# A layer-norm, attention and mixer kernel on one core: the first layer norms staggered by half tiles, segment sums moved from TensorE to VectorE, fewer columns in a product, another last store

## The chip, the cores and the metric

The kernel runs on one core of a Trainium2 chip. The metric is the device time of one execution in microseconds (us). Executions of one kernel spread by a few us (1528.29 to 1531.67 for the kernel before); medians of several are quoted, with the smallest and largest. A profiled execution has a "span", which is about 2 us shorter than the time that the same execution reports (1527.2 against 1529.11 us in the profile before). Runs that lie over 1.5% above the fastest of their kernel would be classed as slow and kept apart.

Engines are named as the profile names them: PE is TensorE (matrix products), PEld its weight loads, DVE is VectorE, ACT is ScalarE, POOL is GpSimd, SP is SyncE, which here only issues DMAs. A "q" after an engine ("SPq", "ACTq") is its queue of DMA issues.

## The reference, cut to what matters

```python
xn = layernorm(x)                                  # x: 2048 x 1024, bf16
out = x + A(xn, mem0, Wq, Wk, Wv, Wo) + B(xn, w1, w2, w3, w4)

def A(x, mem, ...):                                # 64 segments of 32 tokens, 32 heads of 128
    for s in range(64):
        h = concat([mem, x[32*s : 32*s+32]])       # 8 memory rows ahead of 32 tokens
        o = attention(h) @ Wo                      # causal for tokens; memory rows see all 40 rows
        mem = o[:8]                                # the next segment's memory
        outs.append(o[8:])

def B(x, w1, w2, w3, w4):
    h  = gelu(layernorm(x) @ w1)
    hs = shift_four_groups(h) @ w2                 # quarters of h shifted by -1, +1, -2, +2 tokens
    x1 = x + hs
    return x1 + gelu(layernorm(x1) @ w3) @ w4      # 3584 hidden columns
```

The loop over segments is serial. The kernel speculates: attention weights of memory rows are nearly uniform for such data, so the next memory is approximated by the mean of the values of a segment. That mean needs the *sum of the normalised rows of each segment* ("segment sums"), times Wv ("mean-value product"), times Wo ("G product"). All segments then run in parallel, and a test at the end (with a serial loop behind it, which does not run here) guards the guess.

## The kernel before

TensorE runs through these stages (starts on the PE timeline, us): first product with w1 from 9.5; shift product with w2 from 75.1; w3 product from 130.1 and w4 product from 178.9, which alternate in four blocks of 512 tokens; between their groups the mean-value and G products from 203.0; the V product from 542.6; attention from 763.6, that is Q and K projections with small score and output products between; output products to 1521.7.

The loads at the front, and the statistics of a tile (128 rows) for the layer norm of a layer norm:

```python
load_x(0); load_x(1)                       # 256 KB each, SyncE's queue
for c in range(2):                         # w1 in halves
    nc.sync.dma_start(w1_sb[:, :, c * 512:(c + 1) * 512], w1_v[:, :, c * 512:(c + 1) * 512])
    load_x(c + 2)
...
nc.vector.bn_stats(st[:, 0, :], xt[:, 0:512])         # part 0
nc.vector.bn_stats(st[:, 1, :], xt[:, 512:1024])
nc.vector.bn_aggr(mv[:], st[:])
nc.vector.tensor_scalar(ab[:, 0:1], mv[:, 1:2], EPS, None, op0=ALU.add)
nc.vector.tensor_scalar(ab[:, 1:2], ab[:, 0:1], EPS, mv[:, 1:2], op0=ALU.mult, op1=ALU.add)
nc.gpsimd.tensor_tensor(rr[:], ab[:], neghalf[:], op=ALU.pow)
```

The first eight tiles are transposed on TensorE, the others by transposing DMAs. The segment sums are TensorE products too, eight of four columns for each of the 16 tiles:

```python
def seg_sums(n, xn):
    ps = psum0.tile([P, KT, 4], F32, tag="xs")
    for k in range(KT):
        nc.tensor.matmul(ps[:, k, :], xn[:, k * P:(k + 1) * P], segsum[:], start=True, stop=True)
    nc.scalar.copy(xsum[:, :, 4 * n:4 * n + 4], ps[:])
```

The mean-value product works on 71 columns, for the first segment has eight memory rows that all get one value (NQ = 7 + 64):

```python
for hh in range(4):
    for k in range(KT):
        nc.tensor.matmul(ps[:, hh, :], wv[:, k, hh * P:(hh + 1) * P], xb[:, k, :NQ], start=(k == 0), stop=(k == KT - 1))
```

In the w4 stage each tile needs its residual R1 (loaded from memory, x added by POOL, then added to the product by VectorE):

```python
for j in range(4):
    R1, xt = r1s.pop(n); load_r1(n + 1)                        # SyncE's queue
    nc.gpsimd.tensor_tensor(R1[:], R1[:], xt[:], op=ALU.add)
    for ch in range(2):
        ...28 matmuls of 512 columns...
        nc.vector.tensor_tensor(R1[:, half], ps[:], R1[:, half], op=ALU.add)
    # [after tile 0: mean-value products begin]
```

The attention weights Pn of each tile are transposed by a DMA of SyncE's queue into PT. That queue also brings the weights Wq and Wk and the values V, issued in the order of the program. The output product of a tile is scheduled 10 units of the schedule's own clock (roughly us) after its scores:

```python
nc.sync.dma_start_transpose(PTr, Pn[:rows].rearrange("p h k -> p (h k)"))   # 176 of them
...
LAT = 10.0
smalls.append((clock[0] + LAT, ("O", gi_), o_item))
```

The last output is 512 columns wide: an addition by VectorE and a store of 128 KB by SyncE's queue.

Of the kernel before, what the change touches and what calls it, by code (L numbers as in the profile page):

```python
# [77 lines left out]
def kernel(  # L78
# [39 lines left out]

    def const_tile(name, arr):
        d = nc.inline_tensor(_bf(arr), name=name)  # L120
        t = cpool.tile(list(arr.shape), BF16, name=name + "_sb")
        nc.gpsimd.dma_start(t[:], d.ap())
        return t

    ident = const_tile("c_ident", np.eye(P, dtype=np.float32))
    segsum_np = np.zeros((P, 4), np.float32)
    for t in range(P):
        segsum_np[t, t // SEG] = 1.0
    segsum = const_tile("c_segsum", segsum_np)
# [11 lines left out]
    nc.vector.memset(neghalf[:], -0.5)  # L141
    sums = cpool.tile([P, NTILE * 8, 4], F32)
# [41 lines left out]
    with tc.manual_schedule(engines={mybir.EngineType.PE, mybir.EngineType.SP, mybir.EngineType.Pool}), ExitStack() as actx:  # L184
# [6 lines left out]
        with ExitStack() as bctx:  # L191
            w3ctx = bctx.enter_context(ExitStack())
            xctx = bctx.enter_context(ExitStack())
            xsum = xctx.enter_context(tc.tile_pool(name="xs", bufs=1)).tile([P, KT, NSEG], BF16)
# [12 lines left out]
            with ExitStack() as hctx:  # L207
# [7 lines left out]
                with ExitStack() as p0:  # L215
# [13 lines left out]
                    load_x(1)  # L229
                    for c in range(2):  # L230
                        nc.sync.dma_start(w1_sb[:, :, c * 512:(c + 1) * 512], w1_v[:, :, c * 512:(c + 1) * 512])
                        load_x(c + 2)
                    for n in range(4, 7):
                        load_x(n)
# [5 lines left out]
                    def norm_stats(n, part=None):  # L240
# [13 lines left out]
                        nc.vector.tensor_scalar(ab[:, 0:1], mv[:, 1:2], EPS, None, op0=ALU.add)  # L254
                        nc.vector.tensor_scalar(ab[:, 1:2], ab[:, 0:1], EPS, mv[:, 1:2], op0=ALU.mult, op1=ALU.add)
# [4 lines left out]
                    def norm2(n, xn2T, jj):  # L260
                        st, mv, ab, rr, nm2 = stats[n]
                        xn2 = ring.tile([P, D], BF16, tag="xn2")
                        if n < NPE:
                            nc.vector.tensor_scalar(xn2[:], xts[n][:], mv[:, 0:1], rr[:, 1:2], op0=ALU.subtract, op1=ALU.mult)
                        else:
                            nc.scalar.activation(xn2[:], xts[n][:], ACTF.Identity, bias=nm2[:], scale=rr[:, 1:2])
                            nc.sync.dma_start_transpose(xn2T[:, jj], xn2[:])
# [21 lines left out]
                    def seg_sums(n, xn):  # L289
                        ps = psum0.tile([P, KT, 4], F32, tag="xs")  # L290
                        for k in range(KT):
                            nc.tensor.matmul(ps[:, k, :], xn[:, k * P:(k + 1) * P], segsum[:], start=True, stop=True)  # L292
                        nc.scalar.copy(xsum[:, :, 4 * n:4 * n + 4], ps[:])

                    def stage1(n0, nt, xn2T, between):
                        w = nt * P
                        for co in range(KT):
                            ps = psum.tile([P, 512], F32, tag="mm", bufs=4)
                            for k in range(KT):
                                nc.tensor.matmul(ps[:, :w].rearrange("p (n t) -> p n t", t=P), w1_sb[:, k, co * P:(co + 1) * P],  # L300
                                                 xn2T[:, :nt, k, :], start=(k == 0), stop=(k == KT - 1))
# [14 lines left out]
                    for i in range(13):  # L316
                        nc.tensor.matmul(ps[:], wz[:, :P], wz[:], start=(i == 0), stop=(i == 12))
                    norm_stats(0)
                    norm_stats(1, 0)
                    t0 = xn2T_tile()  # L320
                    xn2 = norm2(0, t0, 0)
                    transposes(xn2, t0, 0, 0)
                    transposes(xn2, t0, 0, 1, on_dve=True)
# [3 lines left out]
                    t1 = xn2T_tile()  # L327
                    xn2 = norm2(1, t1, 0)
                    norm_stats(2)

                    def first(xn2=xn2, t1=t1):
                        transposes(xn2, t1, 0, 0)
                        transposes(xn2, t1, 0, 1)
                    xns = {}

                    def sums_of(n):
                        if n in xns:
                            seg_sums(n, xns.pop(n))

                    stage1(0, 1, t0, {3: [first], 4: [lambda: norm_stats(3)]})  # L340
                    groups = [(1, 1)] + [(n, 2) for n in range(2, NT, 2)]
                    tiles2 = {1: t1}
                    xn2s = {}

                    def prep(n):
                        xn2s[n] = norm2(n, tiles2[n - n % 2], n % 2)
                        norm_stats(n + 2)
                        done = range(n - 2, n - 1) if n < NPE else range(NPE - 2, n + 1) if n == NPE else range(n, n + 1)
                        for m in done:
                            xns[m] = norm1(m)  # L350

                    def tr(n, half):
                        transposes(xn2s[n], tiles2[n - n % 2], n % 2, half)


                    for gi, (n0, nt) in enumerate(groups):
                        between = {c: [] for c in range(KT)}
                        if gi + 1 < len(groups) and groups[gi + 1][0] < NPE:
                            m0 = groups[gi + 1][0]
                            tiles2[m0] = xn2T_tile()  # L360
                            prep(m0)
                            between[1] += [lambda m0=m0: tr(m0, 0), lambda m0=m0: prep(m0 + 1)]
                            between[2] += [lambda m0=m0: tr(m0, 1)]
                            between[5] += [lambda m0=m0: tr(m0 + 1, 0)]
                            between[6] += [lambda m0=m0: tr(m0 + 1, 1)]
                        if gi + 2 < len(groups) and groups[gi + 2][0] >= NPE:
                            m0 = groups[gi + 2][0]
                            tiles2[m0] = xn2T_tile()
                            between[2] += [lambda m0=m0: prep(m0)]
                            between[5] += [lambda m0=m0: prep(m0 + 1)]  # L370
                        between[3] += [lambda n0=n0: sums_of(n0 - 1)]
                        between[4] += [lambda n0=n0: sums_of(n0 - 2)]
                        stage1(n0, nt, tiles2[n0], between)
                    for n in range(NT):
                        sums_of(n)
# [29 lines left out]
            with ExitStack() as p3:  # L405
# [5 lines left out]
                m0 = ring.tile([M, D], BF16, tag="m0", bufs=1)  # L411
                nc.sync.dma_start(m0[:], A_mem0[0])
                for _ in range(4):
                    load_w3()
                for c in range(7):
                    nc.sync.dma_start(w4_sb[:, 4 * c:4 * (c + 1), :], w4_v[:, 4 * c:4 * (c + 1), :])

                vbT = big.tile([P, H, NQ + 1], BF16)
                xb = big.tile([P, KT, NQ + 1], BF16)
                gps = []  # L420

                def mem_start():
# [4 lines left out]
                    t0 = ring.tile([P, KT, 1], F32, tag="t0", bufs=1)  # L427
                    nc.vector.tensor_tensor(t0[:], ps9[:, :, M:M + 1], xsum[:, :, 0:1], op=ALU.add)
                    nc.vector.tensor_copy(xb[:, :, 8:NQ], xsum[:, :, 1:NSEG])
# [88 lines left out]
                for tb in range(4):  # L518
# [18 lines left out]
                    for j in range(4):  # L537
# [17 lines left out]
                        if n == NT - 2:  # L555
                            load_wv()
# [440 lines left out]
```

## Time and profile before

| | before |
|---|---|
| time, median of 3 runs | 1529.53 us (1528.29 to 1531.67) |
| span of the profiled run | 1527.2 us |
| PE busy | 1512.6 us, 99% |
| waits of PE in all | about 6 us, nearly all before 20 us |

The engines' busy times on the page of the kernel before (busy us, share of the span, number of instructions):

```profile
PE 1512.6 (99%) x9810; PEld 810.3 (53%) x9883; DVE 530.1 (35%) x1131; ACT 506.8 (33%) x1155; POOL 178.8 (12%) x248
```

TensorE is nearly always busy, so only what shortens its own stream or its waits can show. The waits of PE before (what waited <- engine and tile that ended the wait: us in total, times, longest):

```profile
PE ps L300 <- DMA w_sb<-in_B_w_dram: 2.0, 1, 2.0
PE ps L283 <- DVE xn L264: 1.3, 1, 1.3
...
PE ps L292 <- DVE xnk L273: 0.7, 1, 0.7
```

They are the first half of w1, the first normalised tile, and a segment sum that waits for its input (the line left out is a wait of the warm-up matmuls at the start, of 1.3 us). There is no wait at all for w4. The third cost of the front is the clock. The windows of the kernel before (stretch, length, busy us of each engine, granted TensorE clock, DMA share, GB/s):

```profile
core 0: us, PE busy (x) PEld busy (x) DVE busy (x) ACT busy (x) POOL busy (x), PEclk, DMA share, GB/s
8.00:10.00 2.00, 0.45 (x8) 0.46 (x9) 1.42 (x5) 0.00 (x0) 0.40 (x1) 1.00 1.08 378
10.00:12.00 2.00, 2.00 (x30) 2.00 (x27) 1.66 (x3) 0.83 (x3) 0.40 (x3) 0.69 1.09 394
12.00:14.00 2.00, 1.99 (x20) 1.72 (x19) 1.10 (x5) 1.35 (x3) 0.69 (x1) 0.50 1.06 408
```

PE idled for 2 us until 9.55, and from about 10.8 to 14.2 it ran at half clock (the granted clock was 0.77 from 10.5 to 11.0, 0.50 from 11.0 to 14.0 and 0.82 from 14.0 to 14.5). Before that PE had waited 1.35 us for the first normalised tile and 2.04 us for w1, with eight transposes (0.62 us) between.

Lines of the timeline before (start, us, engine, line, operation): a group of segment sums and what follows it, a group of mean-value products and what follows it, and the tail.

```profile
48.42 0.34 PE L292 MATMUL ps<-c_segsum_sb,xnk 128*128 128x4 bf16 x8
48.62 1.03 PE L300 MATMUL ps<-xn2T,w_sb 128*128 128x256 bf16 x8
...
203.04 1.20 PE L440 MATMUL ps<-xb,wt 128*128 128x71 bf16 x32
204.07 2.11 PE L548 MATMUL ps<-w_sb,h3T 128*128 128x512 bf16 x8
...
1522.16 0.69 DVE L716 TENSOR_TENSOR ot<-pso,Rt 128x512 bf16<-128x512 f32 x1 [6.21 <-PE pso L710]
1522.88 0.36 SPq L717 DMA_DIRECT2D out_dram<-ot  x1
```

Matmuls overlap (the group of segment sums at 48.42 us lasts 0.34 us, and the next work starts 0.20 us after it began), so what a group costs is read from its start to the next start, not from its duration: 0.20 us for a group of segment sums (26 ns for each four-column matmul), 1.03 us for 32 matmuls of 71 columns. From the start of the last addition to the end of the span (1527.2) there are 5.04 us.

### The profile page before, as it was taken

To read this page: it belongs to the slowest core of one execution; us is meant where nothing else is said; L and a number is where in the kernel's file an instruction comes from. 1 tells how busy PE (TensorE), PEld (TensorE's weight loads), DVE (VectorE), ACT (ScalarE), POOL (GpSimd) and SP (SyncE) were. 2 spreads that over 40 slices of the span, in tenths; PEclk is the share of its full clock that TensorE was granted. 3 is DMA by queue.
4 is the path that set the end of the run, shared out by engine and by line. 5 is a ranking of instruction groups with operands and counts; after the bars stand their busy time and mean duration, and the time that the engine had idled before them with its cause. 6 is when DMAs were issued, how large, how long until landed. Compare 5 with 4: busy or idle time off the path is not lost.

```text
span 1527.2 us, 24314 instructions
## 1 busy us (share of the span) xinstructions
PE 1512.6 (99%) x9810; PEld 810.3 (53%) x9883; DVE 530.1 (35%) x1131; ACT 506.8 (33%) x1155; POOL 178.8 (12%) x248
## 2 busy tenths in 40 slices
PE   8999999999999999999999999999999999999998
PEld 7844444444444444444466645654665555445554
DVE  8284010000210122211146624650664266426641
ACT  5533202103012011111156614650663266326620
POOL 5232020221211222100000010001000100010001
PEclk9999999999999999999999999999999999999999
DMA  8679543452352877632399947992997389728611
GB/s 252 186 221 308 208 158 118 142 183 90 115 176 80 213 259 255 223 123 82 125 242 247 235 133 183 234 244 74 229 251 187 106 222 227 183 80 203 177 46 51
DMA packets 287373, 270.03 MB, mean 177 GB/s; under 512 B 136875, under 2 KB 255040, under 8 KB 287000
## 3 DMA queue, kind: packets, MB, share of 16 engines
q1 hardware_dynamic: 265208, 185.79, 47.5%
q0 software_dynamic: 22048, 82.63, 15.5%
q8 instruction: 80, 1.31, 0.4%
q14 instruction: 37, 0.30, 0.1%
HBM read 190.98 MB, written 46.19 MB: 155 GB/s over the span
## 4 chain that ended last, share of the span: by engine, by line
PE 98%; DMA 1%; DVE 0%; issue 0%; ACT 0%; SPq 0%
PE ps L652 30%; PE ps L579 14%; PE pso L710 14%; PE ps L523 13%; PE ps L548 13%; PE ps L387 4%; PE ps L300 3%; PE psS L667 2%; PE psO L691 2%; DMA xt<-in_A_x_dram 1%; PE ps L474 1%; PE ps L837 1%; PE ps L440 1%; PE gps L454 1%; PE ps L292 0%
## 5 line engine op out<-in xcount | busy, mean ns | idle before, releaser
L652 PE MATMUL ps<-hTb,wt 128*128 128x396 bf16 (+3 forms) x2560 | 509.5, 343 | 0.0
L652 PEld LDWEIGHTS <-wt 128*128 128x128 bf16 x2560 | 234.2, 98 | 166.1
L710 PE MATMUL pso<-wo_sb,oX 128*128 128x512 bf16 x1001 | 223.4, 379 | 1.3 <-issue 0.2
L579 PE MATMUL ps<-wt,xT 128*128 128x512 bf16 x1004 | 220.1, 379 | 1.1
L523 PE MATMUL ps<-xn3T,w_sb 128*128 128x512 bf16 x896 | 195.7, 379 | 0.0
L548 PE MATMUL ps<-w_sb,h3T 128*128 128x512 bf16 x872 | 194.3, 379 | 1.2
L579 PEld LDWEIGHTS <-xT 128*128 128x128 bf16 x1024 | 100.2, 98 | 120.8
L524 ACT ACTIVATE h3T<-ps 128x512 bf16<-128x512 f32 x112 | 66.9, 597 | 292.1 <-PE ps L523 291.2
L710 PEld LDWEIGHTS <-oX 128*128 128x128 bf16 x1024 | 98.8, 98 | 115.3
L658 ACT CAST KT<-ps 128x396 bf16<-128x396 f32 (+3 forms) x160 | 82.3, 514 | 224.0 <-PE ps L652 222.5
L548 PEld LDWEIGHTS <-h3T 128*128 128x128 bf16 x896 | 86.8, 98 | 102.8
L523 PEld LDWEIGHTS <-w_sb 128*128 128x128 bf16 x896 | 86.8, 98 | 102.7
L673 DVE TENSOR_REDUCE sums<-sm 99x4 f32<-99x396 f32 (+2 forms) x176 | 97.6, 555 | 113.4 <-ACT sm L671 113.4
L669 DVE TENSOR_TENSOR sm<-psS,c_mask_reg_sb 99x396 f32<-99x396 f32 x160 | 91.3, 571 | 90.2 <-PE psS L667 89.7
L671 ACT ACTIVATE sm<-sm 99x396 f32<-99x396 f32 (+2 forms) x176 | 92.8, 527 | 71.6 <-DVE sm L669 70.9
L581 ACT CAST Vs<-ps 128x512 bf16<-128x512 f32 x64 | 37.4, 586 | 233.3 <-PE ps L579 169.2
L660 ACT ACTIVATE QT<-ps 128x396 bf16<-128x396 f32 (+3 forms) x160 | 84.2, 526 | 74.0 <-PE ps L652 54.1
L585 DVE CAST Vs<-ps 128x512 bf16<-128x512 f32 x64 | 44.3, 692 | 170.0 <-PE ps L579 157.1
L549 DVE TENSOR_TENSOR R<-ps,R 128x512 f32<-128x512 f32 x32 | 22.1, 692 | 232.0 <-PE ps L548 221.1
L679 DVE TENSOR_TENSOR Pn<-sm,rs 99x396 bf16<-99x396 f32 (+2 forms) x176 | 98.9, 562 | 6.3 <-DVE rs L675 0.5
L692 ACT CAST oX<-psO 128x384 bf16<-128x384 f32 (+1 forms) x176 | 82.4, 468 | 8.3 <-PE psO L691 7.8
L717 POOL DMA_DIRECT2D out_dram<-ot x30 | 16.4, 546 | 583.5 <-DVE ot L716 577.6
(118 smaller groups left out, 978.3 us busy)
## 6 DMA issues: line engine op xcount, KB each, us to landing
wt<-in_A_Wk_dram SPq DMA_DIRECT2D x78, 512.0 KB
wt<-in_A_Wq_dram SPq DMA_DIRECT2D x76, 512.0 KB
wt<-in_A_Wv_dram POOLq DMA_DIRECT2D x24, 1024.0 KB, 6.8
V_scratch<-Vs SPq DMA_DIRECT2D x32, 512.0 KB
V<-V_scratch SPq DMA_DIRECT2D x32, 384.0 KB
w_sb<-in_B_w_dram SPq DMA_DIRECT2D x9, 1024.0 KB
R_scratch<-x POOLq DMA_DIRECT2D x16, 512.0 KB, 3.9
R<-R_scratch SPq DMA_DIRECT2D x16, 512.0 KB
```

The costliest lines, as they stand in the source:

```text
L523: nc.tensor.matmul(ps[:].rearrange("p (n t) -> p n t", t=P), w3_sb[:, k, f * P:(f + 1) * P], xn3T[tb][:, :, k, :], start=(k == 0), stop=(k ...
L548: nc.tensor.matmul(ps[:], h3T[:, f, j * P:(j + 1) * P], w4_sb[:, f, ch * 512:(ch + 1) * 512], start=(f == 0), stop=(f == FT - 1))
L579: nc.tensor.matmul(ps[:], xT[:, m4 * 4 + j, k, :], wv[:, k, :], start=(k == 0), stop=(k == KT - 1))
L652: nc.tensor.matmul(ps[:, :nb] if flat else ps[:, :nb].rearrange("p (t c) -> p t c", t=nt), w[:, k, hh * P:(hh + 1) * P], B["rhs"](k), star ...
L658: nc.scalar.copy(o, i)
L660: nc.scalar.mul(o, i, scale)
L669: nc.vector.tensor_tensor(sm[:T, :, :T], S3, t["mask"][:].unsqueeze(1).to_broadcast((T, 4, T)), op=ALU.add)
L671: nc.scalar.activation(e[:T, :, :T], sm[:T, :, :T], ACTF.Exp, scale=LN2)
L673: nc.vector.tensor_reduce(ss, e[:T, :, :T], axis=AX.X, op=ALU.add)
L679: nc.vector.tensor_tensor(Pn[:T, :, :T], e[:T, :, :T], rs[:T, :].unsqueeze(2).to_broadcast((T, 4, T)), op=ALU.mult)
L692: nc.scalar.copy(oX[:, hs_, at:at + nt], O3[:, :, 0:nt])
L710: nc.tensor.matmul(self.ps[:], self.oX[:, h, self.gl * P:(self.gl + 1) * P], wo_sb[:, h, self.cc], start=(h == 0), stop=(h == H - 1))
```

## The change

The intent is to start TensorE earlier and to take small work from its stream. Cut to its core (cuts marked with ...):

```diff
 # front: constants behind w1 (only the identity ahead), w1's first quarter ahead of x1
-    load_x(0); load_x(1)
-    for c in range(2):
-        nc.sync.dma_start(w1_sb[half c], ...); load_x(c + 2)
+    load_x(0)
+    for c0, c1 in ((0, 256), (256, 512), (512, 1024)):
+        nc.sync.dma_start(w1_sb[:, :, c0:c1], w1_v[:, :, c0:c1])
+        if c0 == 0:
+            load_x(1)
 # both variance terms in one operation
-    nc.vector.tensor_scalar(ab[:, 0:1], mv[:, 1:2], EPS, None, op0=ALU.add)
-    nc.vector.tensor_scalar(ab[:, 1:2], ab[:, 0:1], EPS, mv[:, 1:2], op0=ALU.mult, op1=ALU.add)
+    nc.vector.scalar_tensor_tensor(ab[:], epsm[:], mv[:, 1:2], epsa[:], op0=ALU.mult, op1=ALU.add)
 # tile 0 normalised in halves; statistics of tile n+1 staggered by halves; tiles 0 to 3 singly
 # (before: 0 and 1 singly, then pairs); 15 warm-up matmuls in place of 13
+    for n in range(1, NPE):
+        norm_stats(n + 1, 0)
+        norm2_of(n)
+        norm_stats(n + 1, 1)
+        ...
 # segment sums: off TensorE, on to transposing DMAs and VectorE, between the loads of w4
-    nc.tensor.matmul(ps[:, k, :], xn[:, k * P:(k + 1) * P], segsum[:], start=True, stop=True)
+    def seg_sums(n):
+        xr = ring.tile([P, 2, KT, P], BF16, tag="R1", name=f"xp{n}")      # R1's two buffers
+        for j in range(2):
+            nc.sync.dma_start_transpose(xr[:, j], xn_v[:, n + j, :])
+        for j in range(2):
+            nc.vector.tensor_reduce(xb[:, :, 4 * (n + j):4 * (n + j) + 4], ..., axis=AX.X, op=ALU.add)
+    nc.sync.dma_start(m0[:], A_mem0[0])                                    # behind w3, ahead of w4
+    for c in range(8):
+        if c < 7: nc.sync.dma_start(w4_sb[:, 4 * c:4 * (c + 1), :], ...)   # 1 MB each
+        if c > 0: seg_sums(2 * c - 2)
+    seg_sums(NT - 2)
 # 64 columns in place of 71 in the mean-value and G products; memory products after tile 0 of w4
-    ... xb[:, k, :NQ] ...
+    ... xb[:, k, :] ...
 # tail: the last output in two groups of 256 columns; the very last store on ScalarE's queue
+        o = outs.pop()
+        outs += [Out(o.oX, o.gi, o.gl, c0, 256) for c0 in (512, 768)]
+        for o, q in zip(rest[-3:], (nc.sync, nc.sync, nc.scalar)):
+            o.queue = q
```

## The prediction

> **What bounds it.** TensorE. The busy table gives PE 1512.6 of 1527.2 us (99%), and the chain of waits is 98% PE. The list of waits has about 6 us of PE waiting, nearly all in the first 10 us. So the change gains only what it takes from PE's own stream, the first 30 us, or the tail: well under 2%.
>
> **Removed from PE's stream.**
> - Segment-sum matmuls: 16 groups of 8 (4 columns each). In the timeline the next work starts 0.20 us after each group begins: 16 x 0.20 = 3.2 us, all on the chain between 18 and 75 us.
> - 71 to 64 columns in the mean-value and G products (512 matmuls): now about 30 ns each on the chain (7.6 us for 256). The 4-column matmuls show a floor of 0.20/8 = 26 ns[...]. 64 columns should take 27 ns: 512 x 3 ns = 1.5 us.
>
> **The front.** Now PE has transposed tile 0 by 7.5, waits 2.04 us for w1's first half (9.55), runs 4 column blocks, and waits for the second half (12.93). The windows show the granted clock at 0.5 from about 10.8 to 13.9, costing 1.5 us more. [...] After: the first quarter of w1 comes ahead of x1 and the constants' small packets (the DMA row shows 230 GB/s at 4 to 7.5 us, 390 after), so the first product should start near 8.2, set by the second eviction on VectorE. One variance operation less (0.15 to 0.2 us) and halved normalisation (0.55 to 0.3) help little, as POOL's power (0.73) stays. Against it: x2 now follows all of w1, and VectorE takes its statistics before it normalises tile 1; so tile 1's transposes should wait 1 to 2 us at 11 to 14 us, possibly at half clock again. Net front gain 0.5 to 3.3 us; I take 2.
>
> **Moved.** Segment sums: 16 transposing DMAs and 16 VectorE reductions of 1024 elements (estimate 1.15 us each, from 0.57 us for 396) in 137 to 195 us, where VectorE is nearly idle (2.9 of 49 us). Free unless the DMAs delay w4 or R1. Now w4 ends near 163 and is needed from 178.9. The later transposes of the same scratch take about 1.5 us of all queues each (8 in 15.3 us): 16 x 1.5 = 23 us, so w4's last part lands near 180 (needed 184) and R1's first near 192 (needed by 198). It should just fit; I allow 0.4 us on average for stalls.
>
> **Tail.** The last VectorE add falls from 0.69 to about 0.42 us (256 columns; 284 take 0.44), and the last store is halved; two half-width groups cost 0.1 us more on PE. Gain 0.2 to 0.4 us.
>
> **Sum:** 3.2 + 1.5 + 2 + 0.3 - 0.4 = 6.6 us. Predicted 1523.0 us, range 1519.5 to 1526.0. Faster by over 2%: 0.01; within 2%: 0.98; slower: 0.01.
>
> **Right if:** stage 2 (the shift product) starts near 70 instead of 75.1 us; no segment-sum matmul on PE; no PE gap at 179 to 205 us; the first w4 group starts about 5 us earlier; mean-value matmuls about 27 ns apart.
>
> **Wrong if:** the list of waits shows PE waiting for w4, or for xb or R1 at 180 to 210 us (transposes slower than 1.5 us, then up to +5 us); or PE waits over 3 us for xn of tile 1 with the clock halved again, so that stage 2 starts at 72 or later; or the 64-column matmuls stay at 30 ns.

The 27 ns for 64 columns stand as an estimate between the measured 26 ns of four columns and 30 of 71. Two figures are given there without all their numbers. The "0.1 us more on PE" of the half-width groups is 64 matmuls of 256 columns at 109 ns from start to start (50.72 to 60 us in the profile after) against 32 of 512 columns at 215 (256 of them between 75.1 and 129.9 us before). The 1.15 us of a reduction of 1024 elements are an estimate: 0.57 us for 396 elements and 0.86 for 704 (at 1471.5 us before), continued in a straight line, give 1.16; in the change a pair of them took 2.35.

## More of the kernel before

The shift product and the Q and K projections before, by source line (count, ns min/median/max, first and last start). The stretch from the first to the last projection is 691.7 us:

```profile
L387 PE MATMUL ps<-w_sb,hTB x250: 377/379/379, 75.1 to 129.9; 128*128 128x512 bf16 x125
L652 PE MATMUL ps<-hTb,wt x2560: 330/334/386, 763.6 to 1455.3; 128*128 128x396 bf16 x79, 128*128 128x403 bf16 x40, 128*128 128x429 bf16 x39, 128*128 128x495 bf16 x39
```

## The result, and the profile after

| | before | after |
|---|---|---|
| time, median | 1529.95 us (1528.29 to 1531.67, 4 runs) | 1526.71 us (1526.27 to 1530.51, 4 runs) |
| ratio after to before | | 0.9984, 95% interval 0.9965 to 1.0004 |
| span of the profiled run | 1527.2 us | 1524.4 us |

A ratio here and below is the mean time of one kernel's fast runs over the mean of the other's of the same rounds, so it is not quite the ratio of the medians. The time is 3.7 us above the predicted 1523.0 and 0.7 us above the range. A second set of runs of the same kernel (e2 below) gave 0.9981 with an interval of 0.9967 to 0.9995. The second interval leaves out 1, so the gain is real, but small: 2.4 and 2.9 us by the two ratios, well under half of the 6.6 us predicted.

The engines' busy times after:

```profile
PE 1512.6 (99%) x9853; PEld 808.6 (53%) x9853; DVE 545.8 (36%) x1137; ACT 506.7 (33%) x1147; POOL 179.3 (12%) x248
```

Beware of this line: PE is as busy as before, although 128 matmuls have left its stream (98 others came: 64 for the tiles that now go singly, 32 for the split last output, 2 for the warm-up; the PEld counts, 9883 and 9853, agree). Ends of matmuls are modelled, overlapping matmuls count once (the projections after: 509.5 us busy for 2560 matmuls of 343 ns), and some matmul records are missing (9810 recorded before, 9853 after). Starts of stages tell more. The waits of PE after:

```profile
PE psO L689 <- DMA PT<-Pn: 2.2, 2, 1.2
...
PE ps L290 <- DVE xn L271: 1.2, 2, 0.8
PE ps L301 <- DMA w_sb<-in_B_w_dram: 1.0, 1, 1.0
PE ps L301 <- DMA xn2T<-xn: 0.8, 1, 0.8
PE ps L438 <- DVE xb L428: 0.7, 1, 0.7
```

Two waits are shorter (w1, 2.0 to 1.0 us; the first normalised tile, 1.3 to 0.5). Four are new: for the second normalised tile (0.8 of the 1.2 us in the xn line), for a tile transposed by DMA at 50.7 us, for the segment sums (xb) at 200.85, and for transposed attention weights (PT) in the attention stage, which has nothing of the change in it.

The stretch by stretch account (starts on PE, us; every number is one profiled execution):

| start of | before | after | lead of after |
|---|---|---|---|
| first product | 9.55 | 7.91 | 1.6 |
| shift product | 75.1 | 71.7 | 3.4 |
| first w4 group | 178.9 | 175.3 | 3.6 |
| mean-value products | 203.0 | 200.8 | 2.2 |
| V product | 542.6 | 538.7 | 3.9 |
| first Q projection | 763.6 | 759.7 | 3.9 |
| last K projection | 1455.3 | 1453.6 | 1.7 |
| end of output products | 1521.7 | 1520.3 | 1.4 |
| end | 1527.2 | 1524.4 | 2.8 |

Read downwards, the lead is made in the first 75 us, lost in part around 200, won back by the narrower products by 540, lost in the attention, and won back in part by the tail.

The front after. First the windows, then the timeline:

```profile
10.00:12.00 2.00, 0.96 (x18) 0.89 (x16) 0.24 (x1) 0.51 (x2) 1.99 (x7) 1.00 1.07 376
12.00:14.00 2.00, 1.22 (x23) 1.05 (x21) 1.93 (x6) 0.93 (x4) 0.47 (x1) 1.00 1.05 385
```

```profile
7.91 2.17 PE L301 MATMUL ps<-xn2T,w_sb 128*128 128x128 bf16 x32 [0.35 <-ACT xn2T L294]
11.11 1.07 PE L301 MATMUL ps<-xn2T,w_sb 128*128 128x128 bf16 x16 [1.04 <-DMA w_sb<-in_B_w_dram]
11.76 0.69 DVE L256 BATCH_NORM_STATS2 st<-xt 128x6 f32<-128x512 bf16 x1 [2.37 <-DMA xt<-in_A_x_dram]
12.96 0.40 PE L290 MATMUL ps<-c_ident_sb,xn 128*128 128x128 bf16 x4 [0.78 <-DVE xn L271]
```

The clock stays at 1.00 in this execution, with waits of 1.04 and 0.78 us (e14 below is one in which such waits halved it). As predicted, VectorE takes the statistics of tile 2 ahead of normalising tile 1, sits idle for 2.37 us until x2 has landed, and PE waits 0.78 us for tile 1.

Lines of the timeline after that answer to those of before: a transposed tile that came late, the mean-value products, the tail.

```profile
50.72 1.47 PE L301 MATMUL ps<-xn2T,w_sb 128*128 128x256 bf16 x12 [0.85 <-DMA xn2T<-xn]
...
200.85 1.09 PE L438 MATMUL ps<-xb,wt 128*128 128x64 bf16 x32 [0.66 <-DVE xb L428]
201.78 2.54 PE L545 MATMUL ps<-w_sb,h3T 128*128 128x512 bf16 x11
...
1520.57 0.42 DVE L714 TENSOR_TENSOR ot<-pso,Rt 128x256 bf16<-128x256 f32 x1 [3.07 <-PE pso L708]
1521.03 0.38 ACTq L715 DMA_DIRECT2D out_dram<-ot  x1
```

32 matmuls of 64 columns take 0.93 us to the next start, against 1.03 for 71 columns. From the last addition to the end there are now 3.83 us.

How SyncE's queue spends 137 to 195 us after (timeline of SP, an entry's second number is the time that the queue was held; xp is the transposed tile that the segment sums are taken from):

```profile
151.16 5.57 SPq L409 DMA_TRANSPOSE xp<-xn_scratch  x2
156.77 0.58 SPq L418 DMA_DIRECT2D w_sb<-in_B_w_dram  x1
157.52 5.29 SPq L409 DMA_TRANSPOSE xp<-xn_scratch  x2
162.86 0.58 SPq L418 DMA_DIRECT2D w_sb<-in_B_w_dram  x1
...
175.31 15.45 SPq L409 DMA_TRANSPOSE xp<-xn_scratch  x6
190.87 0.51 SPq L513 DMA_DIRECT2D R<-R_scratch  x1
191.42 0.43 SPq L514 DMA_DIRECT2D xr<-in_A_x_dram  x1
```

One pair of transposes and one part of w4 take 6.1 us (156.77 to 162.86), the last six transposes 15.45 us; the residual of the first tile is only issued after them. The chain of waits after, in order of time, from there to the mean-value products:

```profile
191.42 5.56 DMA xr<-in_A_x_dram
...
197.11 2.14 POOL R L541
...
199.88 0.68 DVE R L546
200.56 0.13 DVE MZ L427
200.69 0.11 DVE xb L428
...
200.85 1.09 PE ps L438 x32
```

So PE waits for xb, but the sums themselves were done by 194.3 (VectorE's last reduction). The last operation on xb (adding the memory to the first segment's sum, line 428) stands in VectorE's order behind the residual additions of tile 0, these wait for POOL, and POOL waits for a load that took 5.56 us from its issue.

The shift product and the projections after; the stretch of the projections is now 693.9 us, 2.2 longer, as long as the new waits for PT:

```profile
L375 PE MATMUL ps<-w_sb,hTB x256: 379/379/379, 71.7 to 126.7; 128*128 128x512 bf16 x128
L650 PE MATMUL ps<-hTb,wt x2560: 330/334/385, 759.7 to 1453.6; 128*128 128x396 bf16 x79, 128*128 128x403 bf16 x40, 128*128 128x429 bf16 x39, 128*128 128x495 bf16 x39
```

### The profile page after: what moved, and what is told of

The parts are those of the page before. It is cut to its first block, busy times and chain, and to the rows that moved or that the text cites. A ratio compares the mean times of both kernels' runs of the same rounds, so it can differ in the third digit from the quotient of the medians.

```text
span 1524.4 us, 24352 instructions
## 1 busy us (share of the span) xinstructions
PE 1512.6 (99%) x9853; PEld 808.6 (53%) x9853; DVE 545.8 (36%) x1137; ACT 506.7 (33%) x1147; POOL 179.3 (12%) x248
## 4 chain that ended last, share of the span: by engine, by line
PE 92%; DMA 3%; SPq 3%; DVE 0%; ACT 0%; POOL 0%; issue 0%; POOLq 0%; DVEq 0%; ACTq 0%
PE ps L650 30%; PE pso L708 15%; PE ps L577 14%; PE ps L545 11%; PE ps L522 10%; PE ps L375 4%; PE ps L301 3%; SPq L409 2%; PE psS L665 2%; PE psO L689 2%; DMA PT<-Pn 1%; DMA xp<-xn_scratch 1%; PE ps L837 1%; PE ps L473 1%; DMA xt<-in_A_x_dram 1%; DMA xn2T<-xn 1%
## 5 line engine op out<-in xcount | busy, mean ns | idle before, releaser
L650 PE MATMUL ps<-hTb,wt 128*128 128x396 bf16 (+3 forms) x2560 | 509.5, 343 | 0.0
L708 PE MATMUL pso<-wo_sb,oX 128*128 128x512 bf16 (+1 forms) x1056 | 225.2, 373 | 0.0
L708 PEld LDWEIGHTS <-oX 128*128 128x128 bf16 x1056 | 102.0, 98 | 112.4
L546 DVE TENSOR_TENSOR R<-ps,R 128x512 f32<-128x512 f32 x32 | 21.8, 691 | 200.8 <-PE ps L545 169.2
```

What stands on the lines that cost most here:

```text
L650: nc.tensor.matmul(ps[:, :nb] if flat else ps[:, :nb].rearrange("p (t c) -> p t c", t=nt), w[:, k, hh * P:(hh + 1) * P], B["rhs"](k), star ...
L708: nc.tensor.matmul(self.ps[:, :self.w], self.oX[:, h, self.gl * P:(self.gl + 1) * P], wo_sb[:, h, self.cc], start=(h == 0), stop=(h == H - 1))
```

## The experiments

Fifteen runs were made, all with right results. A comparison of the instruction orders of before and after on every engine showed no difference between the start of the attention and the tail; so the waits in the attention had to come from something else than order. The leading theory on the whole result: the gains of the front, the columns and the tail are about as large as predicted, and the moved sums and a disturbed DMA queue in the attention take a part of them back. Rivals: the gains themselves were smaller (the reordered front worth nothing), or the missing 3.7 us are only spread between executions.

### e1 and e2: both kernels again

No edit.

> The kernel before, unchanged, for a second profile. In the profile of the change, TensorE waited 2.2 us, in two pieces near 800 us, for attention transposes that came late, and 0.85 us at 50 us for a transposed tile of the first norm; before had neither. Theory chance (a transposing DMA is now and then held up by 1 to 2 us, in either kernel, wherever it falls): this profile shows such waits too, or the change's second profile lacks them, and each run's time moves by 1 to 2 us with them. Theory systematic (the change makes them late): here again 0 to 0.3 us of both, and the change's second profile shows both again. Time: 1528 to 1532 us.

> The changed kernel, unchanged, for a second profile and a tighter ratio. Chance: the waits for attention transposes and for tile 11 at 50 us are not at the same places; systematic: 2 us of the first and 0.8 of the second again. Either way the shift product starts at 71 to 72 us, the wait for the vector-sum input at 201 us is 0.5 to 0.8 us again (it follows from order, not chance), and the last VectorE add starts 3.8 us before the end against 5.0 before. Ratio 0.997 to 0.999.

The kernel before took 1530.65 us (1529.56 to 1531.23), ratio 1.0003. It had no wait for w4, xb or PT, and a projection stretch of 691.4 us. The changed kernel took 1527.51 us (1526.7 to 1532.12 in 5 runs), ratio 0.9981 with 0.9967 to 0.9995. Its profile (span 1530.2) was a bad execution, and a telling one. The shift product started earlier than the expected 71 to 72 us, and the wait for xb, of which 0.5 to 0.8 us was expected, was far longer. The waits of PE in e2:

```profile
PE ps L438 <- DVE xb L428: 3.9, 1, 3.9
PE psO L689 <- DMA PT<-Pn: 3.4, 2, 1.9
```

The wait for xb was 3.9 us: the last six transposes held the queue for 19.49 us here (15.45 in the profile after), so R1's x part was issued at 194.98 in place of 191.42. The windows of e2 after it:

```profile
202.00:204.00 2.00, 0.24 (x6) 0.24 (x6) 1.52 (x4) 0.00 (x0) 0.15 (x1) 0.88 0.00 0
204.00:206.00 2.00, 2.00 (x33) 1.71 (x31) 0.00 (x0) 0.00 (x0) 1.93 (x2) 0.50 0.40 162
```

After an idle time of 3.9 us the clock was halved for about 3.1 us of the work (0.50, then 0.77 in the next 2 us). The shift product began at 70.7, 4.8 us ahead of e1, and the mean-value products at 203.8, behind e1's 203.6: all of the lead was gone there. So both profiles of the changed kernel have the waits for xb and PT and neither of before has them, but the size differs much between executions; the late tile at 50.7 us did not come again.

### e3: tile 1 normalised before the statistics of tile 2

```diff
                     for n in range(1, NPE):
+                        if n == 1:
+                            norm2_of(n)
                         norm_stats(n + 1, 0)
-                        norm2_of(n)
+                        if n > 1:
+                            norm2_of(n)
```

> The changed kernel with VectorE normalising tile 1 before it takes tile 2's first statistics (which wait for a later load), in that one place. Theory order: tile 1 is then normalised at about 10.8 instead of 12.9 us, TensorE's wait of 0.8 us at 12 us goes, and single-tile work, and the first pair, start 0.8 to 1.0 us earlier (pair 4 at 26.6 instead of 27.5 us, shift product 0.8 us earlier unless a late transposed tile takes it). Rival, w1: the second half of w1 (11.1 us) and later loads set the pace; the first pair starts at 27.3 or later.

It took 1526.89 us (1525.14 to 1533.29), ratio 0.9988 with 0.9966 to 1.0009, no different from e2. The wait for tile 1 was gone, but the wait for w1's second half was 1.4 us instead of 1.2, and the shift product began at 71.0, against 70.7 in e2. So taking the wait away bought nothing in this execution, in which the loads came later; one profile can't say more. The waits later were there as in the change: PT 2.4, w4 1.2, xb 0.4 us.

### e4: only the tail, on the kernel before

```diff
+        o = outs.pop()
+        outs += [Out(o.oX, o.gi, o.gl, c0, 256) for c0 in (512, 768)]
-        for o in rest[-2:]:
-            o.last = True
+        for o, q in zip(rest[-3:], (nc.sync, nc.sync, nc.scalar)):
+            o.queue = q
```

> The kernel before with only the last output tile split into two halves and the last store on ScalarE's queue. From the start of the last VectorE add to the end of the span, the profiles show 5.04 us before and 3.83 in the change: 1.2 us less, where 0.3 was predicted. If the tail change alone did it, this run shows 3.8 to 3.9 us there, TensorE's own end moves by at most +0.1 us, and the time falls by about 1.1 us; if it came from something else, 4.6 to 5.0 us.

The last addition in the timeline of e4, whose span is 1526.3 us:

```profile
1522.38 0.42 DVE L716 TENSOR_TENSOR ot<-pso,Rt 128x256 bf16<-128x256 f32 x1 [3.07 <-PE pso L710]
```

From there to the end it is 3.92 us, against 5.04 and 5.24 in the two profiles of before, and 3.83 and 3.86 in the two of the change. The tail alone is worth 1.2 us (0.3 was predicted). The narrower addition is 0.27 of it; the other 0.9 lies behind the addition, in the halved store and its other queue, which were not tried apart. The time, 1529.0 us with ratio 0.9996 (0.9981 to 1.0011), can't tell 1.2 us from nothing. The projection stretch was 691.4 us with no wait for PT.

### e5: segment sums back on TensorE, all else as in the change

```diff
+                    def seg_sums(n, xn):
+                        for k in range(KT):
+                            nc.tensor.matmul(ps[:, k, :], xn[:, k * P:(k + 1) * P], segsum[:], start=True, stop=True)
+                        nc.scalar.copy(xsum[:, :, 4 * n:4 * n + 4], ps[:])
...
-                    for j in range(2):
-                        nc.sync.dma_start_transpose(xr[:, j], xn_v[:, n + j, :])
-                        ... tensor_reduce ...
```

> The changed kernel with the segment sums put back on TensorE (128 small matmuls in the first product) and none of the 16 transposing loads and reductions; front, tail and 64 columns stay as changed. Theory (the moved sums cost what they save, by late loads at 150 to 200 us and by what follows in attention): no wait for the vector-sum input or w4, and none for attention transposes (0 to 0.4 us as in the three profiles of before); the shift product starts at 74 to 75 us instead of 70.7 to 71.7; end of span 1522.5 to 1524. Rival (the late attention transposes come from something else in the change): 2 to 3.4 us of waits for attention transposes near 800 us again; span 1525 or more.

The shift product began at 74.6 us, against 71.7 and 70.7 in the change: taking the sums off TensorE is worth 2.9 to 3.9 us there (3.2 predicted). Part of that is chance, since w1's second half landed 0.65 us later in e5; counted from the first transpose of tile 1 it is 3.3 us (61.0 us in e5, 57.7 in e2). Against before's 75.1 to 75.5 the new front alone is worth 0.5 to 0.9 us here (2 predicted); in e10 below it was the same (74.6). In e14 it was worth nothing (76.0), and the clock is why: at tile 1's transposes e14 was level with e5 (13.57 and 13.62), but after waits of 1.21 and 0.79 us its clock was halved from 13.8 to 17.3 us (the longest matmul of its first product took 311 ns, against 273 in e5 and e10 and 314 in before), and it was 1.4 us behind at the shift product. In e5 and e10, with waits of 1.8 to 1.9 and 0.8 us at the same places, it was not halved. There was no wait for w4 and none for xb, so the moved sums are what brings these. But the wait for PT was there, 3.1 us, with a stretch of 696.4 us, so the moved sums are not needed for that one. (The stretch grew by more than the wait because the clock was halved from 806.2 to 809.6 us, after a wait of 1.97 us; by starts on PE this cost about 1.7 us, an estimate: the eight projections at 806.80 took 2.68 us to the next start, where the eight at 809.72 took 1.37.) The time was 1528.29 us (1526.76 to 1530.65), ratio 0.9983 with 0.9967 to 1.0: by time, the change with its sums on TensorE can't be told from the change with its sums moved.

### e6: memory products ahead of tile 0's residual additions

```diff
+                            if n == 0 and ch == 0:
+                                mem_start()
                             nc.vector.tensor_tensor(R1[:, ...], ps[:], R1[:, ...], op=ALU.add)
...
-                        else:
-                            mem_start()
```

> The changed kernel with the memory's first products and their two VectorE operations placed before the first residual add, one row of program order. Theory order (TensorE's wait at 201 us, 0.7 and 3.9 us in two profiles, is for VectorE working in order behind a residual add that waits for R1, loaded after all 16 transposes; the sums themselves are ready at about 190 us): the wait for xb is 0, and any rest is at most 1 us for a PSUM bank. Rival (the sums themselves are late): the wait stays at 0.5 us or more. Attention waits 2 to 3.4 us as in the change.

The wait for xb was 0, but that says little: PE had already waited 6.0 us for the last part of w4, the largest single wait. In the waits of e6:

```profile
PE ps L545 <- DMA w_sb<-in_B_w_dram: 6.0, 1, 6.0
```

That part was issued at 177.72 us behind the transposes and landed at 185.54. The clock was at 0.50 from 186 to 190 us. The times spread from 1524.18 to 1534.59 us (ratio 0.9992, 0.9961 to 1.0023). Whether the order on VectorE matters stays unsettled by this run; that w4 is at risk behind the transposes it shows.

### e7 and e8: eight or sixteen more transposing DMAs that nobody reads

```diff
+                    for _ in range({1: 8}.get(tb, 0)):          # e8: {1: 8, 2: 8}, on the kernel before
+                        nc.sync.dma_start_transpose(dm[:], xn_v[:, 0, :])
```

> The changed kernel with 8 more transposing loads of the same size at about 235 us, into a tile that nobody reads, when the queue has nothing urgent. They change no address of a used tile on purpose and no order in attention; they shift the count of transfers before attention from 187 to 195. Theory phase (where transfers are held up depends on their position in the queue's stream): TensorE's waits for attention transposes are no longer at 798 to 815 us with 2.2 to 3.4 us; they vanish or lie elsewhere. Rival (not position: the timing or the addresses of the changed kernel): 2.2 to 3.4 us at the same two places again.

> The kernel before with 16 more transposing loads of the same size (8 at about 230 us, 8 at about 335 us) into a tile that nobody reads, and w1's first half in two loads: 187 transfers on the queue before the first attention transpose, as in the changed kernel, instead of 170. Segment sums stay on TensorE. Theory phase: waits for attention transposes as in the changed kernel, 2.2 to 3.4 us at 36 to 50 us after attention's start, where before has 0. Rival (addresses, or the timing of the changed kernel): 0 to 0.4 us, as before.

The idea was that the place of an attention transpose in SyncE's queue (the number of transfers ahead of it) decides whether it is late. e8 also has w1 in three loads, as the change has. In e7 the waits for PT stayed (2.2 us in three), in e8 a wait of 0.8 us for PT and one of 0.7 us for QT (the Q projections as ScalarE writes them) appeared on a kernel whose attention is that of before; its stretch was 693.3 us. The times were 1526.18 us (ratio 0.9973, two timed values) and 1529.76 (0.9996). So disturbing the queue of before brings some of the waits, but no rule of the count came out.

### e9 and e10: more distance between scores and output products

```diff
-        LAT = 10.0
+        LAT = 13.0            # e9: the change; e10: the change with sums on TensorE
```

> The changed kernel with one number changed: the scheduler places a score tile's second product at least 13 instead of 10 of its microseconds after the scores. Theory margin (the kernel before had just enough time for its attention transposes, and every kernel whose queue is shifted gets some of them 1 to 2 us late): the waits for attention transposes fall from 2.2 to 3.4 us to 0 to 0.5 us, and the time by 2 to 3 us against the change, to about 1524.5 where no load stall hits at 180 to 205 us. Rival (the transposes are delayed without bound, or the scheduler's longer distance costs as much elsewhere, such as at block ends): the waits stay over 1.5 us or TensorE's attention stretch gets no shorter.

> Segment sums on TensorE as in the earlier such run, with the 13 us distance. No stall left at 180 to 205 us and none in attention: 1525 to 1526 us, 3 us less than the same kernel with 10. If the margin theory is wrong, 1528 again.

The waits for PT were 0 in both. But in e9 another wait took their place:

```profile
PE ps L650 <- DMA wt<-in_A_Wq_dram: 2.8, 4, 1.0
```

In e10 it was 1.3 us. The stretches were 694.6 and 692.5 us, and neither time came down to what was expected. Weights, values and transposes share one queue, issued in order; that the wait went from one of them to another (PT 2.2 to 0, Wq 0 to 2.8 us, after against e9) suggests that the queue as a whole is late, and that whoever needs its next transfer first waits. e9 took 1528.26 us (1526.21 to 1543.32, ratio 1.001, 0.9981 to 1.004), e10 1527.18 (1526.58 to 1529.43, ratio 0.9982, 0.9967 to 0.9996). e10 equals the change in time, with a smaller spread than any kernel with moved sums that was timed more than twice.

### e11: a version meant to beat both

It loads all of w4 and the first residual ahead of the transposes, gives the transposes two small buffers of their own, begins the mean-value products one tile later, and has e3's, e9's and (one tile later) e6's edits.

```diff
+                for c in range(7):
+                    nc.sync.dma_start(w4_sb[:, 4 * c:4 * (c + 1), :], w4_v[:, 4 * c:4 * (c + 1), :])
                 load_r1(0)
+                for n in range(NT):
+                    seg_sums(n)                     # one tile at a time: transpose, then reduce
...
+                            if n == 1 and ch == 0:
+                                mem_start()
```

> The changed kernel with: the 13 us distance; all of w4 and the first residual ahead of the segment sums' transposing loads, which get two buffers of their own; the mean-value products from the third residual tile instead of the second, with the memory's first products ahead of that tile's adds; tile 1 normalised before tile 2's statistics. If the stalls at 175 to 205 us come from loads that queue behind the 16 transposes, and those in attention from too small a margin, TensorE waits for neither xb, w4 nor attention transposes, every execution lies close to the others (no 1530s), and the time is 1521 to 1523 us: the time before less 3.2 (sums), 1.5 (columns), 1.5 to 2 (front), 1.2 (tail). If 1525 or more, something else eats the gain.

It was slower than the change: 1533.56 us (1529.74 to 1535.62), ratio 1.001 with 0.9997 to 1.0023. The waits for w4 and xb were gone, but the 16 transposes now took from 154.96 to 206.4 us, and tile 1's residual, queued behind them, came late: PE waited 3.1 us at 214.65 for VectorE's addition. The waits for Wq were 6.2 us.

### e12 to e15: one transfer more or fewer, early in SyncE's queue

In e12 and e13 the kernel before loads w2, about 55 us before it is needed, by five and by three DMAs in place of four, and nothing else is changed. e14 is e5 and e15 is the change, each with w2 by three.

```diff
-                    for i in range(4):
-                        nc.sync.dma_start(w2_sb[:, 2 * i:2 * i + 2, :], w2_v[:, 2 * i:2 * i + 2, :])
+                    for k0, k1 in ((0, 2), (2, 4), (4, 6), (6, 7), (7, 8)):     # e13, e14, e15: (0, 2), (2, 4), (4, 8)
+                        nc.sync.dma_start(w2_sb[:, k0:k1, :], w2_v[:, k0:k1, :])
```

> The kernel before with one thing changed: w2 is loaded by five DMAs instead of four (the same bytes; its last quarter in two halves), early in the kernel, about 55 us before it is needed. Every later transfer of SyncE's queue thus stands one place further on; nothing else changes, and nothing of the attention. Count theory (attention transposes are late because their place in SyncE's queue has moved): the wait of TensorE for transposed attention weights appears, 0.8 us or more, and the attention stretch is 692.5 us or longer, instead of 0 and 691.4 to 691.7. Rival (the waits come from where and when the data lie, or from the timing of the attention against the rest, and not from the count): no such wait, stretch 691.7 or less, time within 1 us of before's 1530.4.

> The kernel before with w2 loaded by three DMAs instead of four: one place earlier. Count theory: a wait for transposed attention weights of 0.8 us or more, stretch 692.5 us or longer. Rival: none, 691.7 or less.

> The change with the segment sums back on TensorE (as e5), and w2 in three loads, so that SyncE's queue has as many transfers ahead of the first attention transpose as in the kernel before (170, against 171 in e5). Count theory: TensorE's waits for transposed attention weights go from 3.1 us to 0, the attention stretch from 696.4 to 691.5 us, and the time from 1528.3 to about 1524. Rival: they stay at 2 us or more and the stretch at 693 or longer, the time about 1527 to 1528.

> The change with w2 in three loads: 186 transfers ahead instead of 187; 186 is 16 more than before's 170. Count theory with a period of 16: waits for attention transposes fall from 2.2-3.4 us to 0, stretch 691.5, time about 1524.5. Rival: 2 us or more stay, stretch 693 or longer, time 1526.5 to 1527.5.

The wait that never occurred in before or e1 occurred in both shifted copies. A line of the waits of e13:

```profile
PE psO L691 <- DMA PT<-Pn: 1.3, 2, 0.9
```

The projections of e13 ran from 764.5 to 1457.9, a stretch of 693.4 us; e12 had 0.6 us of waits for PT and 692.3 us. The times were 1530.58 us (ratio 1.0005) and 1530.21 (0.9999), which can't resolve a loss of this size. Putting the count back did not help: e14, at before's count, still waited 1.8 us (stretch 693.3, time 1528.03, ratio 0.9985 with 0.9971 to 0.9999), and e15, 16 transfers further (the period that its expectation supposed), 4.3 us for PT (697.5, 1528.42, ratio 0.9986 with 0.9971 to 1.0001). So a change of one transfer, over 700 us earlier, is enough to bring the waits, and the count alone does not decide them.

### The experiments side by side

| profiled run | shift product starts | mean-value products start | projections, stretch | waits of PE for w4 / xb / PT / Wq |
|---|---|---|---|---|
| before | 75.1 | 203.0 | 691.7 | 0 / 0 / 0 / 0 |
| e1 before again | 75.5 | 203.6 | 691.4 | 0 / 0 / 0 / 0 |
| e4 tail only | 75.3 | 203.5 | 691.4 | 0 / 0 / 0 / 0 |
| after | 71.7 | 200.8 | 693.9 | 0 / 0.7 / 2.2 / 0 |
| e2 after again | 70.7 | 203.8 | 695.3 | 0.7 / 3.9 / 3.4 / 0 |
| e3 tile 1 first | 71.0 | 201.1 | 694.3 | 1.2 / 0.4 / 2.4 / 0 |
| e6 memory first | 70.7 | 207.7 | 695.2 | 6.0 / 0 / 3.3 / 0 |
| e7 eight more | 71.7 | 201.7 | 694.2 | 1.2 / 0.3 / 2.2 / 0 |
| e9 distance 13 | 70.8 | 199.6 | 694.6 | 0 / 0.4 / 0 / 2.8 |
| e15 one fewer | 71.5 | 201.3 | 697.5 | 0 / 1.4 / 4.3 / 0 |
| e5 sums on PE | 74.6 | 202.5 | 696.4 | 0 / 0 / 3.1 / 0 |
| e10 e5, distance 13 | 74.6 | 202.7 | 692.5 | 0 / 0 / 0 / 1.3 |
| e14 e5, one fewer | 76.0 | 204.0 | 693.3 | 0 / 0 / 1.8 / 0 |
| e8 before, 16 more | 75.4 | 203.3 | 693.3 | 0 / 0 / 0.8 / 0 |
| e12 before, one more | 76.3 | 204.3 | 692.3 | 0 / 0 / 0.6 / 0 |
| e13 before, one fewer | 76.0 | 204.0 | 693.4 | 0 / 0 / 1.3 / 0 |
| e11 "best" | 70.2 | 210.4 | 699.4 | 0 / 0 / 0.6 / 6.2 |

Three profiles share before's queue up to the tail, and none waits in the attention. All fourteen others do.

The waits for PT are not scattered. In ten profiles (after, e2, e3, e5, e6, e7, e12 to e15) there is one 41.8 to 43.4 us after the first Q projection. It follows a pair of transposes that SyncE's queue takes one after the other; first this pair before:

```profile
798.46 2.83 SPq L682 DMA_TRANSPOSE PT<-Pn  x2
```

And after, with the wait of PE behind it:

```profile
795.47 4.09 SPq L680 DMA_TRANSPOSE PT<-Pn  x2
...
802.28 0.34 PE L689 MATMUL psO<-PT,V 99*128 99x99 bf16 x4 [1.18 <-DMA PT<-Pn]
```

The pair holds the queue for 2.83 us in before, e1 and e4 alike, and for 3.42 to 4.80 us in the eleven other profiles with the distance of 10 (3.42 in e12, whose wait is the smallest). So at this place the disturbed queue is slower each time, which speaks against pure chance; why it is slower there the runs do not show.

## Why the prediction was wrong, point by point

**Segment sums off TensorE: right.** "16 x 0.20 = 3.2 us" was predicted; with and without the sums on TensorE the shift product starts 2.9 to 3.9 us apart (e5 against after and e2), and 3.3 when the chance in w1's landing is taken out.

**Front: the direction right, the size too large.** "Net front gain 0.5 to 3.3 us; I take 2." Step by step it went as described: the first product starts at 7.91 (8.2 predicted), PE waits for tile 1 at 12.96, and the clock was not halved again. But the shift product started 3.4 us earlier in the profile after and 4.8 us in e2 against e1 (5.2 predicted for sums and front); less 3.3 for the sums, the front is worth 0.1 and 1.5 us there, and e5 and e10 show 0.5 to 0.9, e14 none. In the profile after, 0.85 us of it were lost to a tile whose DMA transpose came late at 50.7 us. Two things were missing in the term. Tiles 2 and 3 now go singly: 640 matmuls of the first product against 576, which costs about 0.5 us (an estimate by starts in the profile after: 128 matmuls of 128 columns at 58.8 ns, from 13.86 to 17.15 us, against 64 of 256 columns at 109.1, from 50.72 us). And an early first product is no gain by itself: e8, which has w1 in three loads on the kernel before, began its first product at 8.07 us with the clock at 1.00, 1.5 us ahead of before, but was only 0.4 us ahead at the first segment sum (18.01 against 18.37) and not ahead at the shift product (75.4), since it waited for w1 (1.5 us in two waits) and for a late tile (0.5 us) in between. That the clock stayed up was in part luck, as e14 shows. The wait for tile 1 was foreseen; taking it away (e3) showed no gain in the one profile taken, since w1 came later there. So the front's term was too large, and which of its loads to move next is not settled.

**64 columns: right.** 1.5 us was predicted; the measured 0.10 us for each of 16 groups of 32 makes 1.6, and the lead grows by 1.7 us between 200.8 and 538.7. (A matmul took 29 ns in place of 32, by starts, where 27 and 30 were named; the difference was right.)

**Moved sums: this step failed.** The prediction said "Free unless the DMAs delay w4 or R1", put R1's first load "near 192 (needed by 198)", and allowed "0.4 us on average for stalls". The seven profiles with the sums as the change moves them (after, e2, e3, e6, e7, e9, e15) waited 0.7, 4.6, 1.6, 6.0, 1.5, 0.4 and 1.4 us for w4 and xb together, 2.3 on average, and where one wait was 3.9 us (e2) or 6.0 us (e6) the half clock came on top (0.50 from 204 to 206 and from 186 to 190 us). With the sums on TensorE (e5, e10, e14) these waits were 0. The mis-sized terms are two. The first is the transposes. The prediction counted 1.5 us each, but the number that it gives for it, "8 in 15.3 us", is 1.9 each; sixteen then take 31 us and not 23, and R1 lands near 199 to 200 (an estimate from the prediction's own numbers), later than the 198 by which it was needed. Measured in the profile after: a pair of transposes with a part of w4 took 6.1 us; at the 376 GB/s of the front's windows the 1 MB is 2.8 us, so a transpose costs about 1.6 us (an estimate from these numbers). The last six took about 2.6 each (15.45 / 6); in these 15.45 us the queue waited 2.3 us for VectorE to free a landing buffer and 0.6 us for a transpose to land. The second is what stands behind R1. It was issued at 190.87 (its x part at 191.42) and landed 5.56 us later, at 197.0, even ahead of the 198; but POOL's 2.14 us and VectorE's additions followed, to 200.6, and then the last operation on xb, to 200.8. The condition named under "Wrong if" ("PE waiting for w4, or for xb or R1 at 180 to 210 us") is what came.

**The attention: this failed too, silently.** The sum has no term for the attention, whose instructions do not change; the prediction does not name it at all. The stretch from the first to the last projection grew by 2.2 us in the profile after and by up to 5.8 in e15 (697.5 against 691.7). The runs show three things: the waits come with any of the tried disturbances of SyncE's queue, even one transfer more in the load of w2 (e12, e13); a longer distance takes away the waits for PT and brings waits for Wq (2.8 us in e9, 1.3 in e10), which suggests that the queue as a whole is late; and the count of transfers does not decide it (e14, e15). The place is the same each time, a pair of transposes that holds the queue longer than in before (3.42 to 4.80 us against 2.83). Why the queue of before, of all, runs without a wait is open. That before had been tuned until its queue just fitted would explain it, but it is only argued. Each row is also one execution, and the size of a wait varies between executions of the same kernel (2.2 and 3.4 us in the two profiles of the change).

**Tail: right in direction, too small.** 0.3 us was predicted, 1.2 measured (e4). Only the addition was costed; the store behind it changed more.

**The sum.** In the profile, by the table of leads: 3.6 us ahead at the first w4 group (sums, front), 1.4 us lost by the mean-value products (moved memory products and the wait for xb), 1.7 won by the columns, 2.2 lost in the attention, 0.3 lost in the output products, 1.4 won at the end: 2.8 us of the 6.6 predicted. Step by step, the 3.8 us that are missing in the profile are: 1.8 up to the shift product (3.4 for sums and front against 5.2); 0.8 from there to the mean-value products (1.2 lost against the 0.4 allowed, of which the wait for xb is 0.7); 2.2 in the attention; 0.3 in the output products; less 0.2 for the columns and 1.1 for the tail (1.4 by stage starts, against 0.3). Single executions differ by more than 1 us, so the terms below that are no more than a reading of these two profiles.

## What to carry to other kernels

Work that is taken from the busiest engine was not free here, where it went through a DMA queue that other stages use (2.3 us of waits for w4 and xb on average, 0 with the sums on TensorE): cost the queue to the landing of the last transfer and through the engines behind it (here 9.4 us from R1's issue to TensorE's next group), not to the issue. (How large a margin is enough, no run here tested; e11 shows that moving the loads ahead of the transposes only moved the wait.) When a kernel runs without a single wait in a stage that is fed by one ordered queue, count that as a state without margin and put a term into the sum for losing it: here a load cut into one piece more, over 700 us earlier, was enough (0.6 us of waits in e12). Compare several profiles of a changed kernel before reading a wait from one of them, and look at the store behind the last operation: it was worth 0.9 us here.

## What was measured of the hardware here

- Transposing DMAs were slower than plain loads in this use: about 1.6 us for 256 KB beside w4's loads (estimate above, some 160 GB/s), 15.45 us for six with two landing buffers (2.9 us of it the queue's waits for these), against 376 GB/s for plain loads at the front.
- A load that stood behind transposes in a queue took 5.56 us from issue to landing (R1's x part), against the 0.43 us that the queue is held for its issue.
- A stage fed by one queue began to wait when an early load was cut differently: 0.6 and 1.3 us in e12 and e13, with 0 in three profiles without the shift.
- From the last addition of the kernel to the end of its span it took 5.0 to 5.2 us with 128 KB on SyncE's queue (before, e1), and 3.8 to 3.9 with a narrower addition and 64 KB on ScalarE's (after, e2, e4).
- Four-column matmuls started 26 ns apart (before).
- The clock was halved after idle times of 3.9 us (e2) and 6.0 us (e6), but also after a single wait of 1.97 us (e5), after 1.35 and 2.04 us with only eight transposes (0.6 us) between them (before), and after 1.21 and 0.79 us (e14), while after 1.94 and 0.79 us (e10) it was not halved. So the half clock came also without one long idle time, and waits of about the same size came out either way.
